# Logits in token order, an identity cast on chip, and first values loaded straight to the upper partitions

## The chip, the core and the metric

One core of a Trainium2 chip runs the whole program. The metric is device time in microseconds, lower is better. The engines are TensorE (PE, with its weight loads shown as PEld), VectorE (DVE), ScalarE (ACT), GpSimd (POOL) and SyncE (SP), which here only issues DMAs.

## What is computed

Windowed attention over 8 batches of 576 tokens, 8 heads of 64; four heads look at the last 32 positions, four at every fourth of the last 128 (dilated). Its output, one row of 512 per token, goes through a mixture of 8 experts: logits `x @ w_gate`, a greedy assignment of all (token, expert) pairs in order of falling logit with 576 tokens per expert, then two products per expert.

```python
scores = scale * np.matmul(q, k.transpose(0, 1, 3, 2))
masks = np.stack([mask_plain if h < H // 2 else mask_dil for h in range(H)], axis=0)
attn = np.exp(scores - max); attn = attn / (attn.sum(-1) + 1e-09)
x = np.matmul(attn, v)                       # -> (4608, 512), token by token
...
logits = x @ w_gate
order = np.argsort(-logits.flatten())
for idx in order:
    tok, e = (int(idx) // E, int(idx) % E)
    if assigned[tok] >= 0 or counts[e] >= cap:
        continue
    assigned[tok] = e
    counts[e] += 1
for e in range(E):
    h = np.maximum(x[mask] @ w1[e], 0.0)
    out[mask] = h @ w2[e]
```

## The kernel before

The attention is cut into 32 units: batch b, kind (0 plain, 1 dilated; the dilated heads are stored as four sequences of 144, so that their window is dense too) and a pair of heads ui; unit u is 4 b + 2 kind + ui. For each unit `Unit.build` makes: two `scan` products (L502, L506) for a bound on the maximum, its reduction on DVE (L453), a transpose of that (L458) and a cast (L460); three `scores` products (L513, L518), each with an exponential on ACT (L472); two `values` products (L525, L530) with key blocks of v; and the `weigh` division on DVE (L538 to L540). `banks` then transposes each unit's rows on PE (L589) with the fp32 identity `identf`, ACT keeps the result in `xt` (L287 is the helper `act`), the rows go to HBM by SP (L549).

With the last unit of a batch come the logits of batches 0 to 6: two steps, each of four fp32 products of 288 columns that run side by side in four column groups of PE (L614), one for each pair of heads. They read `xt` in a row, so for the dilated pairs the columns come in the order of the four sequences. An ACT copy brings the lower 64 partitions to `L4`, a DVE copy brings the upper 64 and puts their columns in token order (L622). Transposes (`gates`, L635, L638) and a sum over the four groups (L647) make `Lt`; `R.choose` and `coarse` (L808, L813) prepare the assignment from them. Batch 7 goes another way (`tokens`): per pair of heads one PE step over its tokens in order (L687, L689), for which `text` gives the dilated pairs with a column step of 144 fp32, that is 576 bytes.

V of batch 0 is loaded by three DMAs per kind as pairs of key blocks over all 128 partitions, and then five copies per part and one for the rest (L303, L298) put every key block to partitions 64 to 127 and the half windows around it to 0 to 63. `V_FIRST` gives the engines of batch 0's copies, ACT and DVE; later batches use POOL. The identity `identf` (64 KB) is one of the constants loaded from HBM, in the last group, after the loads of batch 0.

The order on every engine is set by a planner (`Schedule.run`): each step has a cost, its dependencies and a due time, which is the end minus the longest way to the end minus a boost (a larger boost is due earlier); the ready step that is due first goes first, with a tolerance per engine. `D_R` is the rate in bytes per ns by which the planner thinks that loads land. A load that the planner puts beside PE work gets a real wait for a product at that place (`K.gate`), so loads are released by PE's progress. The boost of the logits is `B_K`, -5200; that of the last work on them `B_P`, -105500. What follows the attention, the assignment of the first expert alone (`R.alone`) and eight rounds of expert products, has a planner run of its own.

Of the kernel before, what the change touches and what calls it, by code (L numbers as in the profile page):

```python
# [26 lines left out]
NB = S // 64  # L27
# [13 lines left out]
B_L, B_G, B_T, B_X, B_H, B_HL, B_Y, B_S, B_W = 23000, 27000, 15000, 0, 20000, 17000, 28000, -15000, 1500  # L41
RAW1, D_R, NQ, AHEAD_W = 8, 262, (2, 2), (3, 4)
ADDED, T_A, T_G = (("2", 0), ("1", 1), ("2", 1)), 4500, 4500
V_FIRST = ("ACT", "DVE", "DVE", "ACT", "DVE")
NS, B_E, DIRECT = (2, 2), 3000, 7
# [17 lines left out]
def consts():  # L63
# [38 lines left out]
    f["onesf"] = np.ones((128, 128), np.float32)  # L102
    f["identf"] = eye
    ob, of, cols, fcols = {}, {}, 0, 0
    order = ["ident", "maskm0", "lsel0", "maskm1", "lsel1", "rsel"]
    bf = {n_: bf[n_] for n_ in order + [x for x in bf if x not in order]}
    f = {n_: f[n_] for n_ in ["identf"] + [x for x in f if x != "identf"]}
    for n_, a in bf.items():
# [151 lines left out]
def attention(tc, ctx, C, load_const, T, xd, Lt, R):  # L260
# [28 lines left out]
    def load_v(b, kind, part):  # L289
# [3 lines left out]
        return nc.sync.dma_start(t[:, 4 * part + 1:4 * part + 5:2], T["in_v" + n][b][:, 2 * part:2 * part + 2])  # L293

    def spread(b, kind, part, i, f):
        t = VT[kind][b % 2].rearrange("p c h d -> p c (h d)")
        if part == 2:
            return f(t[32:64, NB - 1], t[64:96, NB - 1])  # L298
        c = 4 * part
        odd, even, behind = (slice(x, x + 3, 2) for x in (c + 1, c, c + 2))  # L300
        o, x = ((t[64:, even], t[:64, odd]), (t[32:64, even], t[:32, odd]), (t[:32, odd], t[32:64, odd]),
                (t[32:64, odd], t[64:96, odd]), (t[:32, behind], t[96:, odd]))[i]
        f(o, x)  # L303
# [96 lines left out]
    def load_values(b, kind):  # L400
        s = b % 2
        oldv = old("v", kind, s)
        done = ready["V", kind, b] = []
        for part in range(3):
            n = 128 * 2 * 4 * 65 * 4 if part < 2 else 64 * 4 * 65 * 4
# [3 lines left out]
            for i in range(5) if part < 2 else (0,):  # L409
                eng = "POOL" if b else V_FIRST[i]  # L410
                f = {"ACT": act, "DVE": nc.vector.tensor_copy, "POOL": nc.gpsimd.tensor_copy}[eng]
                cost = {"ACT": 640, "DVE": 400, "POOL": 660}[eng] // (1 if part < 2 else 2)
                deps = [d, ready["b", kind, s]] + {2: [0, 1], 3: [2]}.get(i, [])
                last[i] = op(eng, cost, lambda part=part, i=i, f=f: spread(b, kind, part, i, f),
                             [last[x] if isinstance(x, int) else x for x in deps], -4 * b * P_U)
                done.append(last[i])
# [158 lines left out]
    def banks(un, xs, done, usex):  # L575
# [7 lines left out]
        for i, (c0, c1) in enumerate(((0, 2), (2, 5))):  # L583
# [12 lines left out]
            late = B_K if b < B - 1 else B_E  # L596
            t = un.op("PE", 109 * (c1 - c0), turn, [*(done if b < B - 1 else done[:i + 1]), *oldt], late, pt, 128)
            usex.append(t)
# [5 lines left out]
        if b >= DIRECT:  # L604
            return tokens(un)
        lg = L4_[b % 2] = []
        sm = []
        base = (b % 2) * S
        for j in range(2):
            pt = Buf(PV)  # L610

            def logits(j=j, pt=pt):
                for g in range(4):
                    nc.tensor.matmul(pt.tile[32 * g:32 * g + 32, :S // 2], wgp[:, g],  # L614
                                     xt_[b, g // 2][0][:, g % 2, 288 * j:288 * j + 288], start=True, stop=True)

            t = un.op("PE", 500, logits, [*xt_[b], ready["w"]], B_K, pt, 32)
            for kk in range(2):
                xt_[b, kk][2].append(t)
            k0 = un.op("ACT", 400, lambda j=j, pt=pt: act(  # L620
                L4.tiles[0][:64, base + 288 * j:base + 288 * j + 288], pt.tile[:64, :288]), [t, *L4_["free"]], B_K)
            k1 = un.op("DVE", 500, lambda j=j, pt=pt: nc.vector.tensor_copy(  # L622
                L4.tiles[0][64:, base:base + S].rearrange("p (t r) -> p r t", r=DIL)[:, 2 * j:2 * j + 2],
                pt.tile[64:, :288].rearrange("p (r t) -> p r t", r=2)), [t, *L4_["free"]], B_K)
            pt.users += [k0, k1]
            lg += [k0, k1]
        c0, c1 = b * S // 128, (b * S + S) // 128
        for c0, c1 in ((c0, c0 + 2), (c0 + 2, c1)):
# [10 lines left out]

            t = un.op("PE", 109 * (c1 - c0), gates, [*L4_[0], *L4_[1]], B_K, pg, 128)  # L640

# [7 lines left out]

            x = un.op("DVE", 60 + 35 * (c1 - c0), settle, [t], B_K)  # L650
            pg.users.append(x)
# [4 lines left out]
        c0, c1 = b * S // 128, (b * S + S) // 128  # L656
        x = un.op("DVE", 800, lambda: R.choose(c0, c1), [x[0] for x in sm], B_K)
        un.op("DVE", 350, lambda: R.bits(c0, c1), [x], B_P)
        coarse(c0, c1, x, B_P)

# [87 lines left out]
    load(0, 0, 0)  # L748
    const(0)
    const(1)  # L750
    ready["r"] = sp(1, choosers, (), 131000, 0)
# [766 lines left out]
def load_consts(tc, pool, T):  # L1518
# [5 lines left out]
    cuts = [(cb, BF, ob, "ident", "lsel0"), (cb, BF, ob, "lsel0", "maskm1"), (cb, BF, ob, "maskm1", "rsel"),  # L1524
            (cf, F32, of, "identf", "pri"), (cb, BF, ob, "tri", None), (cf, F32, of, "pri", None)]
    for i, (src, dt, o, n0, n1) in enumerate(cuts):
# [41 lines left out]
```

## Time and profile before

| | us |
|---|---|
| median of three runs | 684.7 (683.77 to 685.19) |
| profiled execution | 684.89 |
| its span | 683.1 |
| attention, from the start to the last coarse count | 0 to 190.4 |
| the rest | 190.4 to 683.1 |

Busy time counts an engine as busy while any of its instructions runs. In the chain of waits each stretch of the span belongs to the step that the next one waited for.

### The profile page before, as it was taken

What the parts mean: (1) busy time and instruction counts of PE and PEld (TensorE: products, weight loads), DVE (VectorE), ACT (ScalarE), POOL (GpSimd) and SP (SyncE); (2) the same over time, 40 slices, a digit from 0 to 9 for tenths busy, and PEclk for the clock granted to TensorE, in tenths of its full rate; (3) what the DMA queues carried; (4) which work ended last, traced back from release to release, by engine and by line L of the source; (5) the groups of instructions that cost most, each with busy time, mean ns of one, the idle gap of its engine ahead of it and who ended that gap; (6) DMA issues with size and microseconds to landing.
All of it is one profiled execution on the core that took longest, in us unless ns stands there. A gap on an engine that the chain in (4) does not pass through costs nothing.

```text
span 683.1 us, 19154 instructions
## 1 busy us (share of the span) xinstructions
PE 631.4 (92%) x7517; PEld 549.8 (80%) x7517; DVE 467.2 (68%) x1584; ACT 295.7 (43%) x650; POOL 230.9 (34%) x358
## 2 busy tenths in 40 slices
PE   7889898789857999999999999999999999999994
PEld 5777777768644988898799799889879979988983
DVE  6768886687577885689899588778869836614200
ACT  5655455455403835854345145335423525424210
POOL 5568887873004316523203113110320311311011
PEclk9999999999956999999999999999999999999998
DMA  8777787772204937977236116314512744203001
GB/s 251 240 241 248 231 265 239 227 241 74 71 4 141 232 67 200 273 161 233 95 98 216 47 56 207 110 55 139 178 48 79 245 171 147 70 31 102 1 28 42
DMA packets 59099, 99.11 MB, mean 145 GB/s; under 512 B 7424, under 2 KB 26624, under 8 KB 59008
## 3 DMA queue, kind: packets, MB, share of 16 engines
q1 hardware_dynamic: 49664, 72.71, 33.3%
q0 software_dynamic: 9344, 25.17, 13.5%
q8 instruction: 59, 0.97, 0.6%
q14 instruction: 32, 0.26, 0.1%
HBM read 72.69 MB, written 18.87 MB: 134 GB/s over the span
## 4 chain that ended last, share of the span: by engine, by line
PE 54%; DVE 21%; issue 13%; DMA 5%; POOL 3%; ACT 2%; SPq 0%; POOLq 0%; DVEq 0%
PE py L1434 18%; PE ph L1391 17%; DVE xs L540 3%; PE pS L518 3%; PE px L530 2%; PE ptx L1354 2%; PE px L589 2%; DVE mx L453 2%; PE pz L821 2%; DVE hb L1412 1%; PE py L1437 1%; PE py L1439 1%; DVE G L835 1%; POOL out L1460 1%; DMA qs<-in_qd 1%
## 5 line engine op out<-in xcount | busy, mean ns | idle before, releaser
L1434 PE MATMUL py<-w2h,hb 128*128 128x512 f32 x512 | 170.5, 398 | 0.0
L1391 PE MATMUL ph<-xh,w1h 128*128 128x256 f32 (+1 forms) x512 | 138.4, 301 | 0.0
L1391 PE MATMUL ph<-xh,w1l 128*128 128x256 f32 (+1 forms) x512 | 136.4, 297 | 0.0
L1391 PE MATMUL ph<-xl,w1h 128*128 128x256 f32 (+1 forms) x512 | 136.2, 296 | 0.0
L1434 PEld LDWEIGHTS py<-w2h,hb 128*128 128x128 f32 x512 | 96.2, 188 | 19.1
L1460 POOL DMA_INDIRECT out<-y,idx x40 | 40.5, 1013 | 207.6 <-ACT y L1216 144.3
L1216 ACT ACTIVATE hb<-ph 128x256 fp32r<-128x256 f32 (+2 forms) x192 | 59.6, 346 | 105.9 <-PE ph L1391 99.4
L1434 PE MATMUL py<-w2l,hb 128*128 128x512 f32 x256 | 99.9, 390 | 0.0
L303 POOL COPY v<-v 32x520 f32<-32x520 f32 (+1 forms) x140 | 86.9, 625 | 29.3 <-DMA v<-in_vp 14.9
L1391 PEld LDWEIGHTS ph<-xh,w1h 128*128 128x128 f32 x512 | 91.8, 190 | 0.6
L1391 PEld LDWEIGHTS ph<-xl,w1h 128*128 128x128 f32 x512 | 91.6, 190 | 0.0
L1391 PEld LDWEIGHTS ph<-xh,w1l 128*128 128x128 f32 x512 | 91.6, 190 | 0.0
L1412 DVE SCALAR_TENSOR_TENSOR hb<-ph,hb 128x320 fp32r<-128x320 f32 (+1 forms) x128 | 57.2, 453 | 35.2 <-ACT hb L1216 30.7
L472 ACT ACTIVATE E<-pS 128x384 f32<-128x384 f32 x96 | 46.0, 492 | 48.0 <-PE pS L518 43.0
L1216 ACT ACTIVATE y<-py 128x512 f32<-128x512 f32 (+1 forms) x40 | 23.9, 597 | 97.6 <-PE py L1434 83.8
L1434 PEld LDWEIGHTS py<-w2l,hb 128*128 128x128 f32 x256 | 48.2, 188 | 8.5
L1340 POOL DMA_INDIRECT xg<-xd,idx x40 | 41.7, 1043 | 36.5 <-PE ph L1391 25.8
L518 PE MATMUL pS<-q,k 128*64 128x64 f32 x1152 | 53.8, 232 | 0.0
L530 PE MATMUL px<-v,E 128*64 128x65 f32 x1152 | 48.3, 224 | 3.2 <-ACT xt L287 1.1
L1141 POOL TENSOR_TENSOR rx<-oa,const 128x360 bf16<-128x360 bf16 (+2 forms) x9 | 7.0, 778 | 125.4 <-DVE oa L1136 125.4
L530 PEld LDWEIGHTS px<-v,E 128*64 128x64 f32 x1152 | 42.2, 137 | 7.9 <-issue 4.0
L1217 DVE TENSOR_TENSOR xl<-ptx,xh 128x512 fp32r<-128x512 f32 (+1 forms) x36 | 22.9, 636 | 37.2 <-ACT xh L1216 29.2
(203 smaller groups left out, 1135.0 us busy)
## 6 DMA issues: line engine op xcount, KB each, us to landing
raw<-in_moe_w SPq DMA_DIRECT2D x128, 256.0 KB
qs<-in_qp SPq DMA_DIRECT2D x16, 288.0 KB
k<-in_kp SPq DMA_DIRECT2D x16, 288.0 KB
qs<-in_qd SPq DMA_DIRECT2D x16, 288.0 KB
k<-in_kd SPq DMA_DIRECT2D x16, 288.0 KB
v<-in_vp SPq DMA_DIRECT2D x16, 260.0 KB
v<-in_vd SPq DMA_DIRECT2D x16, 260.0 KB
xd<-xs SPq DMA_DIRECT2D x8, 512.0 KB
```

Source lines behind the costliest of these rows:

```text
L303: f(o, x)
L472: e = self.op("ACT", 490, lambda j=j, pS=pS: nc.scalar.activation(self.E[:, 3 * j:3 * j + 3].rearrange("p c x -> p (c x)"), pS.tile[:, :38 ...
L518: x = nc.tensor.matmul(pS[64 * h:64 * h + 64, k, :, h], self.K[:, 32 * g:32 * g + 64], self.Q[:, g], start=False, stop=True, skip_group_ch ...
L530: x = nc.tensor.matmul(px[64 * h:64 * h + 64, c - c0, a], self.E[:, k, 64 * a:64 * a + 64], self.V[:, k, 2 * self.ui + a], start=True, sto ...
L540: nc.vector.tensor_tensor(xs[:, c0:c1, 2 * self.ui:2 * self.ui + 2], px[:, :m, :, :D], rc[:, :, :, None].to_broadcast([128, m, 2, D]), op= ...
L1216: act = lambda o, i, f=AF.Copy: nc.scalar.activation(o, i, f)
L1217: sub = lambda e, o, a, b: e.tensor_tensor(o, a, b, op=OP.subtract)
L1340: nc.gpsimd.indirect_dma_start(out=xg[:n], out_offset=None, in_=xd, in_offset=bass.IndirectOffsetOnAxis(ap=box[0][:n, m:m + 1], axis=0))
L1391: nc.tensor.matmul(o, a[:, d * 128:d * 128 + 128], b[:, d, c0:c1], start=((d, i) == pairs[0]), stop=((d, i) == pairs[-1]))
L1412: hl = op("DVE", 335 if j == 0 else 400, lambda: nc.vector.scalar_tensor_tensor(hb[:, CAP + c0:CAP + c1], o, 0.0, hb[:, c0:c1], op0=OP.max ...
L1434: nc.tensor.matmul(py, x, w, start=(f + i == 0), stop=(f == NF - 1 and i == 2))
L1460: s = nc.gpsimd.indirect_dma_start(out=out, out_offset=bass.IndirectOffsetOnAxis(ap=box[0][:n, m:m + 1], axis=0), in_=y[:n], in_offset=None)
```

## The change

1. The logits step reads the dilated heads with `text`, in token order, as batch 7 does. The result then needs no reordering: one ACT copy of all 128 partitions per step takes the place of the ACT and the DVE copy.
2. `identf` is no longer a constant in HBM: DVE casts the bf16 identity, which is the first constant to land, to fp32. The transposes depend on that.
3. For batch 0, V is loaded so that key blocks land on partitions 64 to 127 at once (`direct_v`: even blocks, odd blocks, the last one), 64 partitions and four blocks a DMA. `shift_v` then copies the half windows to the lower partitions: four copies per kind, two on DVE (five and three blocks), two on ACT (five and four).
4. Batch 6's logits, gates, choice and coarse steps have the boost `B_E + 2 * P_U` (12360) instead of `B_K`, its coarse steps that minus 27 `P_U` (-114000) instead of `B_P`.
5. Numbers of the planner: `D_R` 262 to 290, a transpose 109 to 130 (rows) and 140 (gates).

```diff
-RAW1, D_R, NQ, AHEAD_W = 8, 262, (2, 2), (3, 4)
+RAW1, D_R, NQ, AHEAD_W = 8, 290, (2, 2), (3, 4)
-V_FIRST = ("ACT", "DVE", "DVE", "ACT", "DVE")
...
+    def direct_v(kind, part):
+        n, t = "p" if kind == 0 else "d", VT[kind][0].rearrange("p c h d -> p c (h d)")
+        if part == 2:
+            return nc.sync.dma_start(t[64:, NB - 1], T["in_u" + n][0])
+        return nc.sync.dma_start(t[64:, part:NB - 1:2], T["in_v" + n][0][64 * part:64 * part + 64])
+
+    def shift_v(kind, part, c0, c1, f):
+        t = VT[kind][0].rearrange("p c h d -> p c (h d)")
+        if part == 0:
+            c1 = min(c1, NB - 1)
+            f(t[:32, c0 + 1:c1 + 1], t[96:, c0:c1])
+        else:
+            f(t[32:64, c0:c1], t[64:96, c0:c1])
...
+        if b == 0:
+            done += [sp(1, lambda part=part: direct_v(kind, part), oldv, 64 * (4, 4, 1)[part] * 4 * 65 * 4, b, kind) for part in range(3)]
+            for part in range(2):
+                eng = ("DVE", "ACT")[part]
+                f = {"ACT": act, "DVE": nc.vector.tensor_copy}[eng]
+                done += [op(eng, {"ACT": 255, "DVE": 190}[eng] * (c1 - c0),
+                            lambda part=part, c0=c0, c1=c1, f=f: shift_v(kind, part, c0, c1, f),
+                            [*done[:3], ready["b", kind, s]], 0) for c0, c1 in ((0, 5), (5, NB))]
+            return
...
-            t = un.op("PE", 109 * (c1 - c0), turn, [*(done if b < B - 1 else done[:i + 1]), *oldt], late, pt, 128)
+            t = un.op("PE", 130 * (c1 - c0), turn, [*(done if b < B - 1 else done[:i + 1]), *oldt, ready["i"]], late, pt, 128)
...
+        late = B_K if b < DIRECT - 1 else B_E + 2 * P_U
...
-                                     xt_[b, g // 2][0][:, g % 2, 288 * j:288 * j + 288], start=True, stop=True)
+                                     text(b, g, 288 * j, 288), start=True, stop=True)
...
-            k0 = un.op("ACT", 400, lambda j=j, pt=pt: act(
-                L4.tiles[0][:64, base + 288 * j:base + 288 * j + 288], pt.tile[:64, :288]), [t, *L4_["free"]], B_K)
-            k1 = un.op("DVE", 500, lambda j=j, pt=pt: nc.vector.tensor_copy(
-                L4.tiles[0][64:, base:base + S].rearrange("p (t r) -> p r t", r=DIL)[:, 2 * j:2 * j + 2],
-                pt.tile[64:, :288].rearrange("p (r t) -> p r t", r=2)), [t, *L4_["free"]], B_K)
+            k = un.op("ACT", 400, lambda j=j, pt=pt: act(L4.tiles[0][:, base + 288 * j:base + 288 * j + 288], pt.tile[:, :288]),
+                      [t, *L4_["free"]], late)
...
-            t = un.op("PE", 109 * (c1 - c0), gates, [*L4_[0], *L4_[1]], B_K, pg, 128)
+            t = un.op("PE", 140 * (c1 - c0), gates, [*L4_[0], *L4_[1]], late, pg, 128)
...
-        coarse(c0, c1, x, B_P)
+        coarse(c0, c1, x, B_P if b < DIRECT - 1 else late - u * P_U)
...
+    ready["i"] = op("DVE", 250, lambda: nc.vector.tensor_copy(C["identf"], C["ident"]), [ready["c", 0]], -2e4)
...
-            (cf, F32, of, "identf", "pri"), (cb, BF, ob, "tri", None), (cf, F32, of, "pri", None)]
+            (cb, BF, ob, "tri", None), (cf, F32, of, "pri", None)]
+    C["identf"] = pool.tile([128, 128], F32, name="identf")
```

The new numbers move most of the attention's steps on all engines. Three places follow; line numbers of the changed kernel are up to 18 higher there.

DVE near the start, before: unit 2's second weighing (`rec_123`, 128x4), unit 3's two (`rec_121`), then unit 4's maximum (`mx_119`).

```order
L538 TENSOR_SCALAR rec_123<-px_144 128x4
L539 RECIPROCAL rec_123<-rec_123 128x4
L540 TENSOR_TENSOR xs_126<-px_144,rec_123 128x2x128
L538 TENSOR_SCALAR rec_121<-px_143 128x6
L539 RECIPROCAL rec_121<-rec_121 128x6
L540 TENSOR_TENSOR xs_126<-px_143,rec_121 128x3x128
L538 TENSOR_SCALAR rec_121<-px_145 128x4
L539 RECIPROCAL rec_121<-rec_121 128x4
L540 TENSOR_TENSOR xs_126<-px_145,rec_121 128x2x128
L453 TENSOR_REDUCE mx_119<-pm_139 128x5
L453 TENSOR_REDUCE mx_119<-pm_140 128x4
L460 CAST R<-pm_140 9x128
```

The same place now; `mx_120` is unit 5's.

```order
L556 TENSOR_SCALAR rec_123<-px_145 128x6
L557 RECIPROCAL rec_123<-rec_123 128x6
L558 TENSOR_TENSOR xs_126<-px_145,rec_123 128x3x128
L471 TENSOR_REDUCE mx_119<-pm_140 128x5
L556 TENSOR_SCALAR rec_123<-px_144 128x4
L557 RECIPROCAL rec_123<-rec_123 128x4
L558 TENSOR_TENSOR xs_126<-px_144,rec_123 128x2x128
L471 TENSOR_REDUCE mx_119<-pm_139 128x4
L471 TENSOR_REDUCE mx_120<-pm_140 128x5
L478 CAST R<-pm_139 9x128
```

Unit 4's maximum now stands between unit 2's two weighings, and unit 5's first half ahead of unit 3's weighings.

DVE around the first batch's logits, before: unit 7's maximum (`mx_119`) in two halves, then the cast of its result; L622 are the two copies of batch 0's logits.

```order
L453 TENSOR_REDUCE mx_119<-pm_139 128x5
L622 COPY L_132<-px_143 64x2x144
L622 COPY L_132<-px_145 64x2x144
L453 TENSOR_REDUCE mx_119<-pm_140 128x4
L460 CAST R<-pm_140 9x128
```

The same unit now, from the first half of its maximum to the cast.

```order
L471 TENSOR_REDUCE mx_119<-pm_139 128x5
L478 CAST R<-pm_140 9x128
L471 TENSOR_REDUCE mx_119<-pm_139 128x4
L556 TENSOR_SCALAR rec_123<-px_144 128x6
L557 RECIPROCAL rec_123<-rec_123 128x6
L558 TENSOR_TENSOR xs_125<-px_144,rec_123 128x3x128
L556 TENSOR_SCALAR rec_123<-px_143 128x4
L557 RECIPROCAL rec_123<-rec_123 128x4
L558 TENSOR_TENSOR xs_125<-px_143,rec_123 128x2x128
L478 CAST R<-pm_139 9x128
```

Between the two halves stands the cast of unit 6; after them unit 5's weighings, and no copy of logits.

PE at the end of the attention, before: unit 31's last values (L530), batch 7's second token step (L687, L689; `xt_129` is the plain kind, `xt_131` the dilated), batch 6's gates (L635, L638), unit 30's and 31's transposes (L589).

```order
L530 MATMUL px_145<-v_107,E_117 64x65 x6
L687 MATMUL px_144<-xt_129,wgp 32x128 x4
L689 MATMUL px_144<-xt_129,wgp 32x64
L635 MATMUL px_143<-const_63,L_132 128x128 x2
L635 MATMUL px_145<-const_63,L_132 128x128 x2
L638 MATMUL px_145<-const_63,L_132 64x128
L589 MATMUL px_143<-const_63,xs_127 128x128 x3
L589 MATMUL px_145<-const_63,xs_127 128x128 x2
L589 MATMUL px_143<-const_63,xs_127 128x128 x3
L589 MATMUL px_145<-const_63,xs_127 128x128 x2
L687 MATMUL px_144<-xt_131,wgp 32x128 x4
L689 MATMUL px_144<-xt_131,wgp 32x64
```

The same end now; L830 is batch 6's coarse count, of which one row of sixteen is shown, L607 are the transposes, the first row unit 30's, the others unit 31's.

```order
L548 MATMUL px_144<-v_107,E_117 64x65 x6
...
L830 MATMUL pz<-oh_76,pre_135 128x8
...
L607 MATMUL px_143<-identf,xs_127 128x128 x3
L607 MATMUL px_145<-identf,xs_127 128x128 x2
L607 MATMUL px_144<-identf,xs_127 128x128 x3
L703 MATMUL px_143<-xt_129,wgp 32x128 x4
L705 MATMUL px_143<-xt_129,wgp 32x64
...
L703 MATMUL px_143<-xt_131,wgp 32x128 x4
L705 MATMUL px_143<-xt_131,wgp 32x64
...
L716 MATMUL px_145<-identf,L_132 128x128
L717 MATMUL px_145<-identf,L_132 64x32
```

The gates of batch 6 are gone from here and stand ahead of unit 31's values; unit 30 has one transpose left there, and all four token steps come behind unit 31's transposes.

## Rows read from the trace of the kernel before

**Rows 1.** The page: the span, and the busy time of each engine.

```profile
span 683.1 us, 19154 instructions
PE 631.4 (92%) x7517; PEld 549.8 (80%) x7517; DVE 467.2 (68%) x1584; ACT 295.7 (43%) x650; POOL 230.9 (34%) x358
```

**Rows 2.** Stages: window, length, busy us by engine, clock, DMA share, GB/s.

```profile
0.00:30.00 30.00, 23.25 (x498) 18.66 (x498) 21.68 (x64) 17.24 (x31) 15.02 (x35) 0.89 0.79 240
30.00:160.00 130.00, 112.92 (x3075) 98.51 (x3077) 96.80 (x303) 66.75 (x148) 101.34 (x168) 1.00 0.75 236
160.00:190.40 30.40, 26.28 (x511) 20.20 (x507) 19.88 (x87) 13.69 (x34) 0.97 (x2) 0.97 0.20 61
```

**Rows 3.** Chain of waits, pieces from the attention: start us, us, what.

```profile
42.23 1.19 DVE L L622 x2
...
93.71 1.19 DVE L L622 x2
...
123.46 1.15 DVE L L622 x2
...
126.82 5.63 DMA v<-in_vd
...
144.99 4.49 DMA qs<-in_qd
...
160.98 1.74 DVE L L622 x3
...
173.41 0.67 PE px L614 x8
174.17 0.70 DVE L L622
```

**Rows 4.** Groups, 0 to 190 us: busy us, mean ns, idle before.

```profile
L622 DVE COPY L<-px 64x288 f32<-64x288 f32 x14 | 8.4, 680 | 2.4 <-PE px L614 2.4
...
L303 DVE COPY v<-v 32x520 f32<-32x520 f32 x12 | 5.8, 489 | 0.3
...
L287 ACT ACTIVATE L<-px 64x288 f32<-64x288 f32 x14 | 5.6, 403 | 11.3 <-DVE L L622 7.4 <-PE px L614 3.3
```

**Rows 5.** PE timeline, batch 7's first and third token step: start us, us, line.

```profile
174.33 0.40 PE L687 MATMUL px<-xt,wgp 128*32 128x128 f32 x8
174.55 0.27 PE L689 MATMUL px<-xt,wgp 128*32 128x64 f32 x2
...
184.44 0.64 PE L687 MATMUL px<-xt,wgp 128*32 128x128 f32 x8
184.88 0.40 PE L689 MATMUL px<-xt,wgp 128*32 128x64 f32 x2
```

**Rows 6.** PE timeline, the first transposes; in brackets idle before and releaser.

```profile
19.68 0.76 PE L589 MATMUL px<-const,xs 128*128 128x128 f32 x5 [1.85 <-DMA const<-in_cf]
```

**Rows 7.** Stages of one us after that wait; the clock stands third from the end.

```profile
21.00:22.00 1.00, 1.00 (x34) 0.97 (x30) 0.52 (x2) 0.90 (x2) 0.00 (x0) 0.51 0.55 118
...
23.00:24.00 1.00, 1.00 (x14) 0.55 (x10) 0.83 (x2) 0.95 (x3) 0.94 (x3) 0.50 0.57 182
```

**Rows 8.** Timelines of SP's queue and of ACT near the start.

```profile
12.83 0.33 SPq L384 DMA_DIRECT2D k<-in_kd  x1
...
18.30 1.84 ACT L287 ACTIVATE v<-v 64x520 f32<-64x520 f32 x3 [0.18 <-DMA v<-in_vd]
```

**Rows 9.** Waits, 30 to 160 us: who for whom, us, times, longest.

```profile
DVE q L395 <- DMA qs<-in_qd: 6.6, 5, 3.3
...
PE pm L458 <- DVE mx L453: 5.9, 9, 1.5
```

**Rows 10.** Timelines of DVE and PE at the end of the attention.

```profile
181.73 0.42 DVE L540 TENSOR_TENSOR xs<-px,rec 128x256 f32<-128x256 f32 x1
...
181.47 0.44 PE L635 MATMUL px<-const,L 128*128 128x128 f32 x2
...
182.59 1.92 PE L589 MATMUL px<-const,xs 128*128 128x128 f32 x10
```

More of the change, by code (lines that the diff above doesn't have):

```diff
@@ L102, in consts @@
     f["onesf"] = np.ones((128, 128), np.float32)
-    f["identf"] = eye
     ob, of, cols, fcols = {}, {}, 0, 0
@@ L106, in consts @@
     bf = {n_: bf[n_] for n_ in order + [x for x in bf if x not in order]}
-    f = {n_: f[n_] for n_ in ["identf"] + [x for x in f if x != "identf"]}
     for n_, a in bf.items():
@@ L409, in load_values @@
             for i in range(5) if part < 2 else (0,):
-                eng = "POOL" if b else V_FIRST[i]
-                f = {"ACT": act, "DVE": nc.vector.tensor_copy, "POOL": nc.gpsimd.tensor_copy}[eng]
-                cost = {"ACT": 640, "DVE": 400, "POOL": 660}[eng] // (1 if part < 2 else 2)
+                cost = 660 if part < 2 else 330
                 deps = [d, ready["b", kind, s]] + {2: [0, 1], 3: [2]}.get(i, [])
-                last[i] = op(eng, cost, lambda part=part, i=i, f=f: spread(b, kind, part, i, f),
+                last[i] = op("POOL", cost, lambda part=part, i=i: spread(b, kind, part, i, nc.gpsimd.tensor_copy),
                              [last[x] if isinstance(x, int) else x for x in deps], -4 * b * P_U)
@@ L614, in logits @@
                     nc.tensor.matmul(pt.tile[32 * g:32 * g + 32, :S // 2], wgp[:, g],
-                                     xt_[b, g // 2][0][:, g % 2, 288 * j:288 * j + 288], start=True, stop=True)
-            t = un.op("PE", 500, logits, [*xt_[b], ready["w"]], B_K, pt, 32)
+                                     text(b, g, 288 * j, 288), start=True, stop=True)
+            t = un.op("PE", 500, logits, [*xt_[b], ready["w"]], late, pt, 32)
             for kk in range(2):
                 xt_[b, kk][2].append(t)
-            k0 = un.op("ACT", 400, lambda j=j, pt=pt: act(
-                L4.tiles[0][:64, base + 288 * j:base + 288 * j + 288], pt.tile[:64, :288]), [t, *L4_["free"]], B_K)
-            k1 = un.op("DVE", 500, lambda j=j, pt=pt: nc.vector.tensor_copy(
-                L4.tiles[0][64:, base:base + S].rearrange("p (t r) -> p r t", r=DIL)[:, 2 * j:2 * j + 2],
-                pt.tile[64:, :288].rearrange("p (r t) -> p r t", r=2)), [t, *L4_["free"]], B_K)
-            pt.users += [k0, k1]
-            lg += [k0, k1]
+            k = un.op("ACT", 400, lambda j=j, pt=pt: act(L4.tiles[0][:, base + 288 * j:base + 288 * j + 288], pt.tile[:, :288]),
+                      [t, *L4_["free"]], late)
+            pt.users.append(k)
+            lg.append(k)
         c0, c1 = b * S // 128, (b * S + S) // 128
@@ L648, in settle @@
                     "p (c g e) -> p c e g", c=n, g=4)[:, :, :NE], axis=AX.X, op=OP.add)
-            x = un.op("DVE", 60 + 35 * (c1 - c0), settle, [t], B_K)
+            x = un.op("DVE", 60 + 35 * (c1 - c0), settle, [t], late)
             pg.users.append(x)
@@ L656, in banks @@
         c0, c1 = b * S // 128, (b * S + S) // 128
-        x = un.op("DVE", 800, lambda: R.choose(c0, c1), [x[0] for x in sm], B_K)
+        x = un.op("DVE", 800, lambda: R.choose(c0, c1), [x[0] for x in sm], late)
         un.op("DVE", 350, lambda: R.bits(c0, c1), [x], B_P)
-        coarse(c0, c1, x, B_P)
+        coarse(c0, c1, x, B_P if b < DIRECT - 1 else late - u * P_U)
     def coarse(c0, c1, x, late):
```

## The prediction

> **What bounds the kernel now.** I read four views, in this order. First the page: TensorE is busy 92% of a 683.1 us span [rows 1]. Then the table of stages, because that share is an average [rows 2]: from 190.4 us on the expert products run, which the diff doesn't touch, so what can change is the attention, 0 to 190.4 us, and whatever it gains or loses moves the rest as a block. In its middle, 30 to 160 us, PE has 113 busy us of 130, DVE 97, POOL 101, and DMA 0.75 of its time: nothing is full, four resources wait for one another by turns. So the third view decides, the chain of waits, in which each stretch has one owner [rows 3]: the DVE copy of the logits (L622) owns 1.19 + 1.19 + 1.15 + 1.74 + 0.70 = 5.97 us of it, ten of its fourteen copies; single loads own 5.63 and 4.49 us; the logit products (L614) own one piece of 0.67. Last come groups, waits and timelines of the places that the diff touches.
>
> **The change part by part.** The sum is made against the profiled execution: span 683.1 and 1.79 us around it make 684.89, which is 0.19 above the median of 684.7.
>
> *Logits.* Fourteen DVE copies of 0.60 us net (8.4 / 14; 680 ns each with overlap) go [rows 4]. Fourteen ScalarE copies stay; they grow from 64 to 128 partitions with the same 288 elements in each, so I leave them at 403 ns, and they lose the 7.4 us in which they sat behind L622 [rows 4], which was off the path, as ScalarE idles anyway. What L622 costs is told by its chain share: between 0 (something else is late at once) and -6.0. An example: at 42.23 the two copies stand on DVE between the two halves of unit 7's maximum; the second order place in the section on the change shows that nothing stands there now. What is next late there is PE's own order and, elsewhere, a load. I take half: **-3.0**.
>
> *The strided read.* Token order means that the products for the dilated heads step over 576 bytes from column to column. Batch 7 shows that read already: a step of 128 and 64 columns takes 0.49 us where it reads in a row (174.33 to 174.82) and 0.84 where it steps (184.44 to 185.28) [rows 5], +0.35 for 192 columns, so +0.52 for 288. In the changed step two of four products that run side by side step so; it ends with the slower ones. If the penalty were shared among four it would be half. Fourteen steps: PE gets 3.6 to 7.3 us of work more. How much lies on the path? L614 stands in the chain once [rows 3], which makes the lower end +0.5; with DVE relieved PE will own more of the chain, upper end +7.3. I take four steps of fourteen, near the lower row: **+2.0**.
>
> *Identity.* The first transpose waits 1.85 us for the fp32 identity [rows 6], and after that pause PE was granted half its clock, 0.51 and 0.50 between 21 and 24 us [rows 7], about 1.6 us more. The cast, 128 elements a partition on DVE ahead of unit 0's maximum, is hidden: DVE waited there for PE. One DMA of 64 KB and its issue leave SP. So -3.5 at best. But see what is late next. In the new order unit 3's scan stands ahead of unit 1's values, and its k is issued on SP at 12.83, just ahead of the values that landed at 18.3 [rows 8]; by order of issue it lands at most a little sooner, some 17 to 18 us. PE will stand there instead, long enough that the clock may fall again. At worst 0. I take **-1.0**.
>
> *First values.* Per kind eleven copies become four: DVE six of 489 ns [rows 4], 2.9 us, become copies of 1300 and 780 elements, by the same rate 2.0 us; ScalarE's five become two. They no longer depend on each other but each waits for all three loads, and ScalarE's two of the second kind stand ahead of unit 2's exponentials. Loads keep their bytes and go to 64 partitions instead of 128. Nearest row: ScalarE's values copies start at 18.30 as soon as the load is there and last 1.84 [rows 8], so a load that is late by x delays unit 2 by about x. Bounds -1 to +2; as work saved and waits added are alike, **0**.
>
> The Trainium skill (page "SBUF — State Buffer", section "Door 1: The DMA port swizzle (why `[64,N]` ≈ `[32,N]`)") speaks against this: partitions 64 to 127 are behind 8 of 16 DMA ports, so such a load gets half the bandwidth. No row here shows a 260 KB load to half the partitions. By its 27.2 GB/s a port each of the four loads would take an estimated 1.2 us instead of 0.6, and the sum below would end near 684.4. It is the third rival.
>
> *Order.* New costs and a faster assumed transfer rate (290 for 262) let the planner run ahead: scans stand earlier, as the first order place shows (unit 4's maximum between unit 2's two weighings, and no longer after unit 3's). Gain: PE waits 5.9 us for maxima [rows 9], and an earlier scan hides some. Price: a scan that stands earlier reaches its load sooner, while loads are released by PE's own progress; DVE already waits 6.6 us in five places for q [rows 9]. Bounds -4 and +5, taken **0**.
>
> *Tail.* Batch 6's logits are named "due later", but its boost rises from -5200 to 12360, so they fall due earlier, and the third order place shows it: gates and coarse work of batch 6 leave the end. There the last weighing ends on DVE at 182.15 (181.73 + 0.42), while the transposes of unit 31, the second half of ten from 182.59 that last 1.92, begin near 183.55, as gates from 181.47 and unit 30's stand before them [rows 10]. Now they can begin near 182.2; 0.5 us for the first three, then four token steps of 0.49 + 0.49 + 0.84 + 0.84 end near 185.4. Before, the third step ended at 185.28 [rows 5], then a count and the fourth, 186.3. **-0.9**, bounds 0 and -1.5.
>
> Sum: -3.0 + 2.0 - 1.0 + 0 + 0 - 0.9 = -2.9, so 684.89 - 2.9 = **682.0**.
>
> **The rivals.**
> *One: the strided products become the bound.* All of the 7.3 us land on the path: 682.0 + 5.3 = 687.3, slower. For: DVE gets air, PE is the busiest engine. Against: one L614 piece in today's chain. It decides from the point where over ten of fourteen steps lie on the path (4.9 us of gains / 0.52 is nine, and the noise one more).
> *Two: running ahead meets the loads.* PE is in order; a scan that waits for k holds everything behind it. If eight of the fourteen loads of batches 1 to 7 cost 0.6 us each: +5, 687.0. For: loads own 5.63 and 4.49 us of the chain already [rows 3]. Against: loads are also issued sooner when PE doesn't stall.
> *Three: the values land late.* Twice 1.2 us on the start, in which loads are on the path up to 20 us: 682.0 + 2.4 = 684.4, no change.
> *Four: L622's place is taken.* The chain runs through something as long beside it; -3.0 becomes -0.5: 684.5, no change.
> *Five: every gain holds*, -6.0, -3.5 and some of the -4: 677 to 679.
>
> **How the numbers follow.** The forecast has 0.47, its own range 679.5 to 684; rival one 0.14, two 0.11, three 0.09, four 0.11, five 0.08. Faster or slower means by over 0.2% (1.4 us), about what a measurement of this kernel can tell from no change: below 683.3 or above 686.1. The forecast gives 0.43 to faster and 0.04 to same. Faster: 0.43 + 0.08 = 0.51. Same: 0.04 + 0.09 + 0.11 = 0.24. Slower: 0.25. The range takes in the forecast, rivals three and four and the nearer halves of the others: 677.5 to 688.5.
>
> **What would show it.** Right: the experts begin some 3 us sooner after zero and last as long as before; no L622; the chain share of the ScalarE logits copy is small; the logits products take near 0.5 us more a step; a wait of PE between 15 and 18 us for k in place of the one for the identity. Wrong: PE waits for loads in scans of batches 1 to 4 (rival two), strided products in many pieces of the chain (one), ScalarE's first values starting a microsecond later (three), or a span after 190 us that differs by over 1 us, which no term here allows for.

## The result

The changed kernel took 692.99 us (median of 691.38 to 698.28) against 684.95 beside it: 1.2% slower, ratio 1.0115 (1.008 to 1.015), 8.0 us. Run again on another chip the ratio was 1.0155 (1.0106 to 1.0205). The forecast was 682.0 with a range up to 688.5, so the sign was wrong and the range too.

The profiled execution took 693.38 us. Its page, the span, the busy times and the chain by engine:

```profile
span 691.6 us, 19123 instructions
PE 639.9 (93%) x7513; PEld 555.0 (80%) x7516; DVE 460.2 (67%) x1563; ACT 295.1 (43%) x644; POOL 232.2 (34%) x358
PE 53%; DVE 15%; issue 13%; DMA 10%; POOL 5%; ACT 2%; SPq 0%; POOLq 0%; DVEq 0%; ACTq 0%
```

DVE's busy time fell by 7 us, as the edit says [rows 1], and its share of the chain is now 15% (21% before). What came in its place is DMA: 10% of the chain, 5% before. The chain of the kernel before:

```profile
PE 54%; DVE 21%; issue 13%; DMA 5%; POOL 3%; ACT 2%; SPq 0%; POOLq 0%; DVEq 0%
```

Within the attention the chain's pieces that DMA owns add up to 48.5 us, where before had 23.3. The stages (window, length, busy us by engine with instructions, clock, DMA share, GB/s) tell where:

```profile
0.00:30.00 30.00, 23.41 (x553) 19.34 (x556) 20.48 (x61) 16.34 (x26) 14.03 (x35) 1.00 0.89 243
30.00:160.00 130.00, 113.49 (x2883) 96.57 (x2883) 90.82 (x283) 62.88 (x137) 96.45 (x159) 0.95 0.75 233
160.00:199.20 39.20, 34.72 (x647) 26.63 (x643) 19.96 (x89) 17.37 (x44) 6.36 (x11) 0.98 0.18 54
199.20:691.60 492.40, 468.32 (x3440) 412.48 (x3440) 328.95 (x1132) 198.55 (x439) 115.38 (x155) 0.97 0.40 120
```

Against [rows 2]: the start is ahead, 553 products for 498, at full clock for 0.89. The middle loses: in the same 130 us PE issues 2883 products instead of 3075, although its busy time is the same. Two things stretch that busy time: the clock granted is 0.95 instead of 1.00, and the logits products, which now step, take 11.2 us of this stretch instead of 5.8. Neither explains the missing products by itself: without the step (e1_row below) PE is 6 us less busy and issues no more of them. Everything that was not done there stands in the end, 39.2 us for 30.4. The experts take 492.4 us, as before. So the whole loss, 9 us in this execution, is in the attention, and its cause lies between 30 and 160 us.

Four of the waits of that stretch (who for whom, us, times, longest):

```profile
DVE q L406 <- DMA qs<-in_qd: 12.0, 7, 3.9
ACT q L284 <- DMA qs<-in_qd: 11.4, 6, 4.6
POOL v L314 <- DMA v<-in_vd: 7.7, 4, 4.9
ACT q L284 <- DMA qs<-in_qp: 5.3, 5, 1.3
```

DVE waits 12.0 us for loads of q, 6.6 before [rows 9]. One such wait from end to end: SP issues the loads of batch 7's dilated q at 149.28, DVE copies them when they have landed, at 155.35, after standing for 3.94 us, and PE's scan (the tail of a group that began at 152.66) stands for 3.79 us behind that copy. Timelines of SP's queue, of DVE and of PE:

```profile
149.28 1.01 SPq L393 DMA_DIRECT2D qs<-in_qd  x2
```

```profile
150.99 0.42 DVE L471 TENSOR_REDUCE mx<-pm 128x4 bf16<-128x256 f32 x1
155.35 0.45 DVE L406 COPY q<-qs 64x576 f32<-64x576 f32 x1 [3.94 <-DMA qs<-in_qd]
```

```profile
152.66 0.35 PE L520 MATMUL pm<-const,const 128*64 128x320 bf16 x2
156.81 0.36 PE L524 MATMUL pm<-k,q 128*64 128x64 bf16 x10 [3.79 <-DVE rec L556]
```

PE's row names DVE's `rec` as the last to come, but DVE had stood idle from 151.41 to 155.35, and its own row has the cause: the load. The stages of one us behind it:

```profile
156.00:157.00 1.00, 0.19 (x10) 0.30 (x11) 0.92 (x4) 0.93 (x2) 0.00 (x0) 1.00 1.09 374
157.00:158.00 1.00, 1.00 (x25) 0.91 (x19) 0.96 (x2) 0.81 (x2) 0.00 (x0) 0.58 0.40 137
158.00:159.00 1.00, 1.00 (x26) 0.96 (x26) 0.58 (x3) 0.00 (x0) 0.00 (x0) 0.50 0.12 40
159.00:160.00 1.00, 1.00 (x26) 1.00 (x25) 0.52 (x2) 0.29 (x1) 0.15 (x1) 0.50 0.43 121
```

After the pause PE works, but at half its clock (0.50, the lower level, 1.2 GHz). Here the wait is paid twice. Before, the middle had no such row (1.00 in [rows 2]).

### The profile page after: what moved, and what is told of

The parts are those of the page before. It is cut to its first block, busy times and chain, and to the rows that moved or that the text cites. A ratio compares the mean times of both kernels' runs of the same rounds, so it can differ in the third digit from the quotient of the medians.

```text
span 691.6 us, 19123 instructions
## 1 busy us (share of the span) xinstructions
PE 639.9 (93%) x7513; PEld 555.0 (80%) x7516; DVE 460.2 (67%) x1563; ACT 295.1 (43%) x644; POOL 232.2 (34%) x358
## 4 chain that ended last, share of the span: by engine, by line
PE 53%; DVE 15%; issue 13%; DMA 10%; POOL 5%; ACT 2%; SPq 0%; POOLq 0%; DVEq 0%; ACTq 0%
PE py L1451 16%; PE ph L1408 16%; PE px L548 4%; DMA qs<-in_qd 3%; PE pS L536 3%; PE ptx L1371 2%; POOL xg L1357 1%; DVE hb L1429 1%; PE px L607 1%; POOL out L1477 1%; DMA k<-in_kp 1%; PE pz L838 1%; PE pm L524 1%; PE px L633 1%; DVE G L852 1%
## 5 line engine op out<-in xcount | busy, mean ns | idle before, releaser
L1477 POOL DMA_INDIRECT out<-y,idx x40 | 42.7, 1067 | 205.7 <-ACT y L1233 141.7
L536 PE MATMUL pS<-q,k 128*64 128x64 f32 x1152 | 55.5, 235 | 0.0
L548 PE MATMUL px<-v,E 128*64 128x65 f32 x1152 | 51.1, 231 | 0.6 <-issue 0.5
L548 PEld LDWEIGHTS px<-v,E 128*64 128x64 f32 x1152 | 45.0, 144 | 5.4 <-issue 1.6
```

The costliest lines, as they stand in the source:

```text
L536: x = nc.tensor.matmul(pS[64 * h:64 * h + 64, k, :, h], self.K[:, 32 * g:32 * g + 64], self.Q[:, g], start=False, stop=True, skip_group_ch ...
L548: x = nc.tensor.matmul(px[64 * h:64 * h + 64, c - c0, a], self.E[:, k, 64 * a:64 * a + 64], self.V[:, k, 2 * self.ui + a], start=True, sto ...
L1477: s = nc.gpsimd.indirect_dma_start(out=out, out_offset=bass.IndirectOffsetOnAxis(ap=box[0][:n, m:m + 1], axis=0), in_=y[:n], in_offset=None)
```

## The experiments

Ratios are to the kernel before on the same chip, with 95% intervals; 0.001 is 0.69 us. "Attention" is the end of the last coarse count in the profiled execution (190.05 before, 199.21 after). It shows where time went, but it is of one execution, and executions of one kernel differ by several us: c1_tok and b276 end it at 195.34 and 198.81 at ratios of 1.000 and 1.0031. Where the two disagree, the ratio counts.

### Is it the stepped read of the logits?

**e1_row**, the changed kernel with the logits read in a row:

```diff
-                                     text(b, g, 288 * j, 288), start=True, stop=True)
+                                     xt_[b, g // 2][0][:, g % 2, 288 * j:288 * j + 288], start=True, stop=True)
```

> The changed kernel with one thing undone: the logits products read all heads in a row again. The order on every engine stays word for word that of the changed kernel. (The logits of the dilated heads then stand in the order of the four sequences, so the assignment is another; the amount of work is the same.) Theory A, the column step of 576 bytes puts its whole price on TensorE's path (the seven places where the logits stand took 14.9 us in the changed kernel, 8.6 before, so 6.3 us): 693.0 - 6.3 = about 687. Theory B, the new order meets its loads and the step is covered by waits that are there anyway: 692 to 693.

Measured 1.0106 (1.0066 to 1.0147), attention 199.19. **e2_step** is the opposite edit on the kernel before:

> The kernel before with one thing changed: the logits products read the dilated heads with the column step of 576 bytes; the copies behind them stay, and so does the order on every engine, word for word. (DVE's copy then permutes the dilated heads' columns once more, so the assignment is another; the amount of work is the same.) Theory A: 14 steps of 0.45 us more, all on the path, 684.9 + 6.3 = about 691. Theory B: the step is covered as my forecast had it, 0.5 to 2 us on the path, 685.4 to 687.

Measured 1.0052 (1.0021 to 1.0084), +3.6 us; attention 191.21. The groups of the logits products (busy, mean ns), of the changed kernel, of e1_row, of the kernel before and of e2_step:

```profile
L633 PE MATMUL px<-xt,wgp 128*32 128x288 f32 x112 | 15.4, 542 | 0.0
```

```profile
L633 PE MATMUL px<-xt,wgp 128*32 128x288 f32 x112 | 8.5, 412 | 0.7 <-issue 0.7
```

```profile
L614 PE MATMUL px<-xt,wgp 128*32 128x288 f32 x112 | 8.6, 414 | 0.0
```

```profile
L614 PE MATMUL px<-xt,wgp 128*32 128x288 f32 x112 | 15.4, 543 | 0.0
```

The step costs PE 6.9 us in the changed order and 6.8 in that of before, 0.49 for each of fourteen. In the order of before about half of that reaches the time by the ratio (1.2 us by the attention of the one execution); in the changed order none shows: e1_row ends its attention where the changed kernel does, and in the middle it issues as few products:

```profile
30.00:160.00 130.00, 107.35 (x2873) 94.94 (x2869) 88.66 (x283) 63.21 (x137) 97.69 (x160) 0.95 0.75 234
```

Theory A, that the step is the loss, falls.

**f1_part1** has all of part 1 in the order of before; the planner still counts the DVE copies, so nothing else moves (its stepped read is the edit of e2_step):

```diff
...
-            k0 = un.op("ACT", 400, lambda j=j, pt=pt: act(
-                L4.tiles[0][:64, base + 288 * j:base + 288 * j + 288], pt.tile[:64, :288]), [t, *L4_["free"]], B_K)
+            k0 = un.op("ACT", 400, lambda j=j, pt=pt: act(
+                L4.tiles[0][:, base + 288 * j:base + 288 * j + 288], pt.tile[:, :288]), [t, *L4_["free"]], B_K)
-            k1 = un.op("DVE", 500, lambda j=j, pt=pt: nc.vector.tensor_copy(
...
+            k1 = un.op("DVE", 500, lambda: None, [t, *L4_["free"]], B_K)
```

> The kernel before with part 1 alone, in the order of before: the logits products step, ScalarE copies all 128 partitions, the fourteen DVE copies are gone; what is left stands in the same order on every engine (the planner still counts the DVE copies). The run with the step alone took 688.4 against 685.2 beside it, so about +3.2. My sum gave the copies -3.0 (bounds 0 and -6.0). If they were worth their chain share: 688.4 - 3.0 = about 685.4; if nothing, because something else is late at once: 688.4; if all of it: 682.4.

Measured 1.0036 (1.0005 to 1.0067), attention 190.91. Against e2_step the copies' removal gives 0.0016, 1.1 us, with an uncertainty of some 3 us; the attention of the two profiles differs by 0.3. **c1_tok** takes the step away by another road (`text` then returns every head in a row, and one copy a step is left; the planner counts the longer copies, so the order moves too):

```diff
...
+                o, h = xt[:, ui].rearrange("p (t r) -> p r t", r=DIL), S // DIL
+                for r0, r1, t0, t1 in ((0, 1, 0, h), (1, 2, 0, 112)) if c0 == 0 else ((1, 2, 112, h), (2, 4, 0, h)):
+                    i = h * r0 + t0 - 128 * c0
+                    act(o[:, r0:r1, t0:t1], pt.tile[:, i:i + (r1 - r0) * (t1 - t0)].rearrange("p (r t) -> p r t", r=r1 - r0))
...
```

> The kernel before with part 1 done in another place: ScalarE writes the dilated heads' rows into xt in token order (four pieces for each pair of heads, with a column step on the write side, in place of two), so TensorE reads every head in a row, one ScalarE copy a step, no DVE copy; batch 7's steps read in a row as well. If the step on TensorE was the price (3.2 us measured) and the copies are worth 0 to 3: 1.000 to 0.995, and the tail's two stepped token steps give back 0.35 each, so about 0.7 us more. If ScalarE's 32 extra pieces land on the path: 1.00 to 1.005.

Measured 1.000 (0.9976 to 1.0025): no gain. No run shows a gain from part 1.

### Are the other parts worth what the sum said?

**f2_ident** (identity cast alone, order of before):

```diff
...
-            (cf, F32, of, "identf", "pri"), (cb, BF, ob, "tri", None), (cf, F32, of, "pri", None)]
+            (cb, BF, ob, "tri", None), (cf, F32, of, "pri", None)]
+    C["identf"] = pool.tile([128, 128], F32, name="identf")
...
+                if (u, c0) == (0, 0):
+                    K.ops[-1].fn = lambda f=K.ops[-1].fn: (nc.vector.tensor_copy(C["identf"], C["ident"]), f())
```

> The kernel before with the identity cast alone, in the order of before: one cast more on DVE ahead of unit 0's maximum, one DMA of 64 KB less on SP, everything else word for word in its place. My sum gave -1.0, with bounds -3.5 and 0: about 684. The rival: the wait of 1.85 us before the first transposes only becomes another one, or what it gains is given back at the next load: 685.

Measured 0.999 (0.9958 to 1.0022), attention 190.84. PE's timeline has the first transposes without a wait, half a us earlier than in [rows 6], and nothing is left of that at the end:

```profile
19.20 0.55 PE L589 MATMUL px<-identf,xs 128*128 128x128 f32 x3
```

**e7_first** (part 3 of the change alone, its diff as in the section on the change):

> The kernel before with the first values alone (64-partition loads straight to the upper half, four copies a kind; the planner moves the rest a little). My term: 0 (-1 to +2). Rival three, the values land about 1.2 us later per kind (in the changed kernel the plain kind's last one landed at 11.72 us, before at 10.55): +1 to +2.4, ratio 1.002 to 1.0035. If nothing waits for them: 1.000.

Measured 0.9998 (0.9971 to 1.0024). ScalarE's first dilated values do start later than in [rows 8], by 1.07 us in the changed kernel and by 3.04 in e7_first (21.34), but the time of e7_first shows nothing of it. ScalarE's timeline in the changed kernel:

```profile
19.37 2.24 ACT L284 ACTIVATE v<-v 32x1300 f32<-32x1300 f32 x2 [0.24 <-DMA v<-in_vd]
```

**e8_late6** (part 4 alone, its diff as in the section on the change):

> The kernel before with the due times of batch 6's logits alone (the planner moves the whole end, and a little more). My tail term: -0.9 (bounds 0 and -1.5), so 684. A rival: the work of batch 6 that leaves the end stands ahead of units 28 and 29 instead, and nothing is gained or the experts begin later: 685 to 688.

Measured 1.0022 (0.9986 to 1.0059). Its last weighing (DVE) and last coarse count (PE):

```profile
184.32 0.42 DVE L540 TENSOR_TENSOR xs<-px,rec 128x256 f32<-128x256 f32 x1
```

```profile
189.73 1.00 PE L814 MATMUL pz<-oh,pre 128*128 128x8 bf16 x10 [1.72 <-DVE pre L809]
```

From the last weighing to the end are 190.73 - 184.74 = 5.99 us, where before had 190.05 - 182.15 = 7.90 [rows 10]. In this one execution the tail is 1.9 us shorter, but the weighing comes 2.6 us later: batch 6's work stands ahead of it now.

### Is it the planner's rate?

**e3_262** is the changed kernel with `D_R` 262, **e4_290** the kernel before with 290, **b276** the kernel before with 276; one number each.

> The changed kernel with the planner's transfer rate set back from 290 to 262 bytes per ns; everything else stays, so the order moves. Theory A: the rate doesn't matter, 692 to 693.5. Theory B (the planner believes in loads that come sooner than they do, and puts products ahead of their data; the loads on the chain rose from 5% to 10% of the span's chain): most of 5 us back, 688 to 689.

> The kernel before with the planner's transfer rate alone set from 262 to 290. Theory A: within 1 us of 684.9. Theory B: TensorE stands in front of loads as in the changed kernel, 688 to 690.

> The kernel before with the planner's rate at 276, half way between 262 (ratio 1) and 290 (1.015). If the loss follows how late the loads are released, it lies between: 1.003 to 1.012. If 290 was one unlucky order among many, 276 can come out anywhere, also below 1.

Measured: e3_262 1.0035 (1.0007 to 1.0062), e4_290 1.015 (1.0115 to 1.0185), b276 1.0031 (1.0005 to 1.0058). So the rate alone costs the kernel before 10 us, as much as the whole change (8.0 us, and 10.7 when it was run again), and taking it back in the changed kernel returns most of the loss.

The rate does two things: it moves the order, and it moves the releases. A load waits on the chip for the product which the planner has ending last by the time at which it places the load. A batch's fourteen loads (eight of 288 KB, four of 260, two of 65) are 3.56 MB, 13.6 us at 262 bytes per ns and 12.3 at 290, so by the end of a batch the planner believes in data an estimated 1.3 us sooner, and leaves that much less of PE's work between a release and its first reader. The chip moved 236 GB/s in the middle, stores and all [rows 2], below either.

### The order, or the moment of release?

These runs keep an order word for word and name another product for the loads to wait for. **e11_gate** is the changed kernel with

```diff
-                self.gate = next((m for e, m in reversed(self.marks) if e <= t + 200), None)
+                self.gate = next((m for e, m in reversed(self.marks) if e <= t - 2800), None)
```

> The changed kernel, in its own order on every engine, word for word; only the product for which a load waits is another: one that the planner has ending 3 us earlier. If the loads are late because the faster assumed rate releases them later against TensorE's progress, most of the loss comes back: 686 to 688. If the loads are bound by bandwidth or by their buffers, so that an earlier release only shifts the queue: 692 to 694. If the loss isn't in the loads at all: 693.

Measured 1.0033 (1.0003 to 1.0063), attention 189.55 instead of 199.21, and 34.9 us of DMA in its chain instead of 48.5. To have the changed kernel on a second chip, **a_again**:

> The changed kernel itself once more, beside the others of this batch on one chip: ratio to the kernel before 1.0115 as first measured (1.008 to 1.015). If the loss depended on the chip, it would leave that interval.

Measured 1.0155 (1.0106 to 1.0205), attention 198.81.

The other direction, in the order of before. **g1_late** (`t + 3200` in the line above):

> The kernel before, in its own order on every engine, word for word; each load waits for a product that the planner has ending 3 us later. If the moment of release is the cause by itself: a loss like that of the changed kernel, ratio 1.008 to 1.016. If it only hurts together with scans that run ahead: 1.000 to 1.004.

Measured 0.9998 (0.9966 to 1.003), but it tests nothing: when the planner places a load, a later product is mostly not there yet to be named, so only about a third of the releases moved, and over all of them the mean shift is some 0.35 us of the plan. **h1_late** names the product afterwards:

```diff
...
+                self.planned = t
...
+                for w in [w for w in self.late if w[1] < t + x.cost]:
+                    self.late.remove(w)
+                    self.after_(w[0], next(m for e, m in reversed(self.marks) if e <= w[1]), "transfers keep step with the products")
...
-                return after(i, K.gate, "transfers keep step with the products")
+                K.late.append((i, K.planned + 1700))
+                return
```

By this edit a few small transfers at the very end of the attention lose their wait for a product; for the others the named product ends 1.5 us later in the mean of the plan.

> The kernel before, in its own order on every engine, word for word; each load waits for a product that the planner has ending 1.5 us later (this time named after the fact, so that it moves). If the moment of release is the cause by itself: a loss, 1.005 to 1.015, as many us as with 1.5 us earlier were gained (6) or more. If it only hurts with scans that run ahead: 0.999 to 1.003.

Measured 1.0156 (1.0104 to 1.0209), attention 198.52. Its stages, the waits of the middle, and its chain:

```profile
0.00:30.00 30.00, 22.18 (x479) 17.79 (x481) 19.69 (x60) 16.88 (x30) 12.60 (x31) 0.89 0.72 218
30.00:160.00 130.00, 109.75 (x2886) 94.63 (x2884) 92.93 (x289) 64.20 (x143) 96.85 (x158) 0.99 0.78 235
160.00:198.50 38.50, 33.79 (x718) 27.63 (x718) 25.09 (x105) 15.71 (x38) 8.66 (x15) 0.96 0.23 70
```

```profile
POOL v L307 <- DMA v<-in_vp: 19.3, 7, 4.9
ACT q L291 <- DMA qs<-in_qd: 11.6, 6, 2.4
DVE q L402 <- DMA qs<-in_qd: 9.9, 5, 3.5
ACT q L291 <- DMA qs<-in_qp: 9.2, 4, 3.0
```

```profile
PE 47%; DVE 17%; issue 14%; DMA 12%; POOL 5%; ACT 3%; SPq 1%; POOLq 0%; DVEq 0%; ACTq 0%
```

With nothing changed but the releases, the kernel before shows the changed kernel's picture: 2886 products in the middle (2883 there, 3075 in [rows 2]), DVE waiting 9.9 us for q, DMA 12% of the chain (49.0 us of it in the attention, 48.5 in the changed kernel), an attention that ends at 198.5. The clock is not what makes this loss: the middle has 0.99 here. **g3_early** (`t - 1300`) and **h2_early3** (`t - 2800`) go the other way:

> The kernel before, in its own order, each load released at a product that the planner has ending 1.5 us earlier. If it still waits for loads that are released too late (the two of 5.63 and 4.49 us in its chain): 0.993 to 0.998. If its loads are bound by bandwidth and buffers: 1.000.

> The kernel before, in its own order, each load released at a product that the planner has ending 3 us earlier; 1.5 us earlier gave 0.991. If each microsecond of earlier release still takes waits away: 0.984 to 0.988. If 1.5 us took them all: 0.990 to 0.992. If transfers that come too early get into each other's way: above 0.993.

Measured 0.991 (0.9878 to 0.9941) and 0.9927 (0.99 to 0.9953). Stages of g3_early:

```profile
0.00:30.00 30.00, 24.03 (x514) 18.85 (x515) 22.25 (x67) 18.02 (x33) 18.08 (x41) 1.00 0.83 257
30.00:160.00 130.00, 116.57 (x3095) 101.95 (x3094) 96.56 (x309) 68.34 (x149) 98.41 (x163) 0.97 0.75 235
160.00:186.40 26.40, 23.05 (x472) 18.50 (x469) 16.60 (x79) 11.60 (x29) 0.00 (x0) 0.99 0.19 58
```

So in one and the same order, by release: 1.5 us later 1.0156, as it was 1, 1.5 us earlier 0.991, 3 us earlier 0.9927. The loss is steep on the late side, and on the early one 3 us bring no more than 1.5. g3_early, 680.6 us against 685.5 beside it, beats both kernels by that one number.

### With the loads out of the way

> The changed kernel in its own order, loads released 3 us earlier (alone: ratio 1.0033), and the logits read in a row. (The dilated heads' logits stand in the order of the four sequences, so the assignment is another; the work is the same.) If the step's price was hidden under waits for loads, it shows now that they are gone: 1.0033 - 0.0046 = about 0.999. If the changed order hides it in any case: 1.003.

**g2_row** (the edits of e11_gate and e1_row together): 0.9994 (0.9961 to 1.0027), attention 189.49. Its middle, and that of e11_gate:

```profile
30.00:160.00 130.00, 112.66 (x3041) 98.99 (x3042) 95.62 (x306) 68.10 (x150) 100.49 (x166) 0.99 0.75 238
```

```profile
30.00:160.00 130.00, 118.97 (x3052) 100.19 (x3051) 94.46 (x305) 69.18 (x151) 101.12 (x166) 0.99 0.76 239
```

Without the step PE is 6.3 us less busy in the middle and does no more products. The ratio moved as expected, but by less than its uncertainty, and the attention ends at the same time. What hides the step there, with the loads early, isn't settled.

> The changed kernel (rate 290, its costs) with loads released 3 us earlier and the dilated heads' rows written into xt in token order by ScalarE, so that TensorE reads in a row everywhere; the planner moves the order a little. With the step's 3 us and the late loads gone, what is left of the change are the gains of my sum (copies, identity, tail, and 0.7 us of batch 7's steps): 0.994 to 0.999. If those gains are not there: 1.000.

**g4_both**: 0.9985 (0.9956 to 1.0014), attention 189.93. Once its loads are early, the changed kernel is level with the kernel before as it was. But early has to be compared with early: with its loads 3 us early the kernel before takes 0.9927, the changed kernel 1.0033 (e11_gate), 0.9994 without the step (g2_row) and 0.9985 as g4_both. That is 4 to 7 us more, with intervals that do not meet, though from different chips. So the late release, which gave most of the loss, is not all that the change costs; what the rest is, the new order or its other parts, no run here separates.

## Why the prediction was wrong

**What bounds the kernel** held: four resources that wait for one another, loads owning the longest pieces [rows 3]. The conclusion drawn from it was too narrow. I priced what the edits add to engines, when the middle runs on a balance of releases and products.

**The order term is the step that failed.** I put it at 0 between -4 and +5. It is worth +5.5 to +8.4 in the changed kernel, which had 1.0115 and 1.0155: with the old rate it has 1.0035, with early release in its own order 1.0033. In the order of before the rate alone costs 10 us (1.015), late release alone 10.7 (1.0156). My text had the fact ("loads are released by PE's own progress") and the change of `D_R`, and treated the rate as something that reorders scans. It sets the lead that each load gets. Rival two was the nearest, but for half of the mechanism: scans that run ahead of their loads; in h1_late no scan stands earlier than before, and the loss is as large. Its price, eight loads of 0.6 us, was too small too: single waits reach 3.9 to 4.9 us, and in the changed kernel the clock adds to them. My point against it, "loads are also issued sooner when PE doesn't stall", left out that a stalled PE also releases the next loads later.

**Logits, -3.0**: not found, though not excluded either. f1_part1 against e2_step gives -1.1 with some 3 us of uncertainty, c1_tok nothing. Rival four (something else is late at once) fits best.

**The stepped read, +2.0**: its size was right, 0.49 us a step for 0.52, and in the order of before +3.6 (1.4 to 5.8) holds my value. Rival one, that it decides the sign, falls by e1_row.

**Identity, -1.0**: the wait went as foreseen and the clock was 1.00 up to 30 us; but f2_ident gives -0.7 with 2.2 of uncertainty, and its attention ends no sooner. The wait for k that I put in its place did not come at that size: the changed kernel's PE timeline has unit 2's scan waiting 1.48 us for its mask, and unit 3's 0.24 for k.

```profile
14.55 0.33 PE L520 MATMUL pm<-const,const 128*64 128x320 bf16 x2 [1.48 <-DMA const<-in_cb]
...
16.90 0.35 PE L524 MATMUL pm<-k,q 128*64 128x64 bf16 x10 [0.24 <-DMA k<-in_kd]
```

**First values, 0**: held, 0.9998. Rival three's mechanism is there: the packets of batch 0's V (1040 bytes each) take 83 ns in the mean in the changed kernel, 52 before. The Trainium skill (page "SBUF — State Buffer", section "Door 1: The DMA port swizzle (why `[64,N]` ≈ `[32,N]`)") gives loads to half the partitions half the bandwidth; the trace agrees in kind. The plain kind's last load lands at 11.72 instead of 10.55, about what rival three priced, the dilated kind's last packet ends only 0.2 us later (18.90, 18.67 before), and the time shows neither. The 1.07 us by which ScalarE starts later are no measure of it, as its copy now waits for all loads of its kind and before for one.

**Tail, -0.9**: the mechanism is there and larger. In the changed kernel the last weighing (DVE) and the last count (PE) leave 199.21 - 192.68 = 6.5 us, 7.9 before:

```profile
192.26 0.42 DVE L558 TENSOR_TENSOR xs<-px,rec 128x256 f32<-128x256 f32 x1
```

```profile
198.21 1.00 PE L830 MATMUL pz<-oh,pre 128*128 128x8 bf16 x10 [1.72 <-DVE pre L825]
```

It shows no gain, though: what left the end stands ahead of it (e8_late6: 1.9 us shorter, begun 2.6 later, ratio 1.0022). I counted the work that goes from the tail and not where it goes.

**Together**: e3_262, all parts at the old rate, is +2.4 us (0.5 to 4.2). The single parts give +2.5, -0.7, -0.1 and +1.5, which is +3.2. The rate takes it from there to 8 or 10.7. Of "what would show it", no L622, steps of half a us and the unchanged experts came true, and so did the sign of rival two: loads of k that scans waited for stand in the chain with 4.24 us from 43.29, 4.35 from 52.85 and 4.65 from 63.77, beside those of q. Not settled: what the order at 290 costs beside its releases (e3_262 and e11_gate end level, but early against early something is left), and why neither the copies nor the step matter in the changed order.

## What to carry to other kernels

Where transfers are released by the progress of an engine, the lead of a release is a quantity of its own: read it in the trace (issue, landing, first reader), and move it by itself before trusting any edit that moves the order. A planner's constant for a transfer rate is not a number of the order only; here it is an estimated 1.3 us of lead in a batch, and 1.5 us of lead were 11 us of time one way and 6 the other. A gain on an engine that waits for others by turns should be taken as zero until a run with the order held still shows it.

## What was unexpected

A wait for a load can cost PE twice. After the 3.79 us of the example above PE ran at 0.58, 0.50 and 0.50 of its clock. With the loads 3 us earlier (e11_gate) the middle's mean is 0.99, where the changed kernel has 0.95 in the same order. It is the smaller price, though: h1_late loses as much at 0.99, and g3_early, the fastest, has 0.97.

The loss is lopsided: in the order of before, 1.5 us of lead less cost 10.7 us, 1.5 more gained 6.2, 3 more 5.0; the last two can't be told apart.

A step of 576 bytes between the columns that PE reads raises a group of fp32 products of 288 columns from 412 to 542 ns in the mean (half of its products step), and 6.9 us of PE work can leave no mark on the time.
